# Branch transform of 64 by 32 points in place of 128 by 16, its first stage as pairs of matmuls of 64 rows

## The chip, the cores and the metric

The kernel runs on one core of one Trainium2 chip. The time is device microseconds of one execution; three runs of the kernel before gave 1190.42, 1190.47 and 1191.18 us (median 1190.47). The engines are TensorE (PE; its weight loads are shown apart as PEld), VectorE (DVE), ScalarE (ACT), GpSimd (POOL) and SyncE (SP, which only issues transfers here). Everything is computed in 32-bit numbers; matmul operands are split into a rounded part and a remainder, so that a product takes three matmuls (high by high, high by low, low by high).

## The reference

Two kinds of layers alternate, each added to its input `x` (2048 rows of 576 channels). The first is a Fourier transform over rows and channels, of which the real part is kept. The second, the branch, is a long convolution along the rows, done through a transform of twice the length:

```
def _B_ref(q, k, v, shift_k, ssm_k, ssm_D):
    ...
    kv = k_shift * v                      # short convolution of k (4 taps), times v
    kv_f = rfft(pad(kv)); kf_f = rfft(pad(ssm_k))
    y = irfft(kv_f * kf_f)[:S] + kv * ssm_D
    return q * y

x = A_x
x = x + _A_ref(_layernorm(x), ...)
x = x + _B_ref(_layernorm(x), B_k, B_v, B_shift_k, B_ssm_k, B_ssm_D)
x = x + _A_ref(_layernorm(x), ...)
x = x + _B_ref(_layernorm(x), B_k, B_v, B_shift_k, B_ssm_k, B_ssm_D)
```

The branch's convolution does not depend on `x`, only the gate `q` does. So the kernel computes `y` once, beside the first Fourier layer, and uses it twice.

## The kernel before

The Fourier layer (`layer`) runs over steps: for each block of 512 output rows (`tb`) and each of two matrices (`g`), 16 steps `k`. A step multiplies one 128-row slice of the normed input (tile `mats`) by a matrix slice of 128 by 512 that is loaded from `c_mat`, split by ScalarE (L94) and VectorE (L95) and used by 14 matmuls of 512 columns: three for each of four accumulators (`s`) and two for the remaining channels (`rm`). `load_c` asks for the slice of the step after next, so splits run two steps ahead.

The branch (`branch`, a generator) is advanced by hand between half steps, up to step `F1_END` = 42 in its first stage. Its transform of the 2048 points (odd frequencies of the double length) is worked out as 128 points by 16. Stage one (`f1_products`) takes, for each of 16 residues `j` and for each source `src` (1 the filter `ssm_k`, 0 the signal `kv`), a tile of 128 rows by 576 channels, split into two parts `xf`, and multiplies it by cosines and sines (`fc`, from `f1c`, 128 by 4 times 128: two outputs `c`, high and low part). Per half of the channels and per output there are three matmuls of 288 columns over 128 rows into one PSUM bank (`bank()`, a ring of three, name `bk`); ScalarE copies it out (L454) and the pair of outputs is stored to `t_d` in DRAM (L455). The signal's rows come from `convolve`, long VectorE operations on 1152 columns (L398, L403), which are spread over the items of stage one. The operands of stage one (`xf`, `fc`) lie in one tile, `f1r`; the constants come by POOL's queue (`load_fr`, L172), the first of them by SP and a ScalarE copy (L419, L420).

The middle stage (`mid_half` and the functions beside it) reads `t_d` in groups of 128 partitions, four outputs by 16 residues by real and imaginary part, does the 16-point transform, the product with the filter's transform and the inverse, and stores to `v_d`. The last stage (`i2_products`) reads rows of `v_d`, multiplies by `i2c` (six matmuls of 128 rows per half row) and stores `yb_d`. The order on each engine is the program's order as far as the scheduler of the framework leaves it; it moves instructions ahead of others where operands are late.

Of the kernel before, what the change touches and what calls it, by code (L numbers as in the profile page):

```python
# [10 lines left out]
F32 = mybir.dt.float32  # L11
FR = mybir.dt.float32r
AF = mybir.ActivationFunctionType
OP = mybir.AluOpType

P = 128
S = 2048
D = 576
J = S // P
TB = 4  # L20
NT = 512
HD = D // 2
NC = 4
REM = D - NC * P
EPS = 1e-5
# [16 lines left out]
MW = 504  # L42
# [25 lines left out]
def fnet_h3_kernel(ctx: ExitStack, tc: tile.TileContext, x, c_mat, w_re, w_im, k_pad, v, shift_k,  # L68
                   ssm_k, ssm_d, f1c, i2c, midc, out):
    nc = tc.nc  # L70
# [3 lines left out]
    dr = ctx.enter_context(tc.tile_pool(name="dr", bufs=1, space=bass.MemoryType.DRAM))  # L74

    def mm(ps, lhsT, rhs, first, last, more=False):
        nc.tensor.matmul(ps, lhsT, rhs, start=first, stop=last, skip_group_check=more)  # L77

    def bank():
        return psp.tile([P, NT], F32, tag="b", bufs=3, name="bk")  # L80
# [83 lines left out]
    anchor, made, rounded, pows, biased, halved, added, evac, parted, stored = [], [], [], [], [], [], [], [], [], []  # L164

    def load_after(dst, src):
        with tc.issue_after(anchor[-1]):
            return nc.sync.dma_start(dst, src).ins
# [31 lines left out]
        made.append(nc.vector.tensor_tensor(t[:, D + REM:], y[:, :NC * P], h[:, :NC * P], OP.subtract).ins)  # L200
        return t

    t_d = dr.tile([P, J, 2, 2, D], F32, name="t")
    v_d = dr.tile([P, J, 2, D], F32, name="vd")
    yb_d = [dr.tile([P, D], F32, name=f"yb{j}") for j in range(J)]
    xa_d = [dr.tile([P, D], F32, name=f"xa{j}") for j in range(J)]
    xb_d = [dr.tile([P, D], F32, name=f"xb{j}") for j in range(J)]
# [144 lines left out]
    def quads(v):  # L352
        return v.rearrange("p (a q) -> p a q", a=4)

    def branch():
        f1r = region_b(FR, "f1r")
        lay(f1r, 0, ("xf", 2 * D, 3), ("fc", 4 * P, 5))
        at = lay(flts, SC_AT + CRAW * NT, ("so", D, 4), ("land", D, 3))
        lay(flts, at, ("craw", NT, 1))
        f1f = region_a(F32, "f1f")  # L360
        ks = f1f[:, :KR * 2 * D]
        lay(f1f, KR * 2 * D, ("wt", 2 * D, 2), ("rp", 2 * D, 2))
        tmp = f1f[:, 8 * 2 * D:]
        wt, rows, landed, fcs = [], {}, {}, {}
# [8 lines left out]
        def load_k(upto):  # L373
            while k_loaded[0] < min(upto, (J + 4) // 2):
                i = k_loaded[0]
                at = i % KR * 2 * D
                nc.sync.dma_start(ks[:, at:at + 2 * D],
                                  bass.AP(tensor=k_pad.tensor, offset=k_pad.offset + 2 * i * D,
                                          ap=[[J * D, P], [1, 2 * D]]))
                k_loaded[0] += 1  # L380

        def k_rows(row):
# [28 lines left out]

        def f1_const(j):
            if j not in fcs:
                fcs[j] = quads(ring["fc"]())
                if pows:
                    load_fr(fcs[j], f1c[j])
                else:
                    raw = quads(tmp[:, :4 * P])
                    nc.sync.dma_start(raw, f1c[j])  # L419
                    nc.scalar.activation(fcs[j], raw, AF.Copy)  # L420

# [23 lines left out]
        def f1_products(j, src, xf, fc):  # L445
            for hf in range(2):
                so = two(ring["so"]())
                cs = slice(hf * HD, (hf + 1) * HD)
                for c in range(2):
                    ps = bank()  # L450
                    mm(ps[:, :HD], fc[:, c, :], xf[0][:, cs], True, False)
                    mm(ps[:, :HD], fc[:, c, :], xf[1][:, cs], False, False)
                    mm(ps[:, :HD], fc[:, 2 + c, :], xf[0][:, cs], False, True)
                    stored[:] = [nc.scalar.activation(so[:, c, :], ps[:, :HD], AF.Copy).ins]  # L454
                nc.scalar.dma_start(t_d[:, j, :, src, cs], so)  # L455
                yield

        conv, made_ops, split_up, share = convolve(), 0, [], 0.0
        for n, (j, src) in enumerate(todo):
# [3 lines left out]
            xf = f1_split(j, src)  # L463
# [48 lines left out]

        RW = D - MW
        per = MW // RW
        groups = P // 4
        mids = [(q, 1) for q in range(groups)] + [(q, min(per, groups - q)) for q in range(0, groups, per)]

        def width(n):
# [3 lines left out]
        def load_mid(n):  # L522
            if n < len(mids):
                first, count = mids[n]
                w = width(n)
                landed[n] = [r[:, :w] for r in apart] if n % 2 else [ring["land"]()[:, :2 * w]]
                ends = landed[n] if n % 2 else [two(landed[n][0])[:, i] for i in range(2)]
                src = t_d[4 * first:4 * (first + count)]
                if n < groups:
                    src = src.rearrange("q j c s d -> (q j c) s d")[:, :, :MW]  # L530
                    if n % 2:
                        for i in range(2):
                            load_after(ends[i], src[:, i])
                    else:
                        load_after(two(landed[n][0]), src)
                else:
                    src = src.rearrange("(g q) j c s d -> (q j c) s g d", q=4)
# [41 lines left out]
        def mid_inverse(n, yf):  # L579
            w = width(n)  # L580
            pv = bank()
            mm(pv[:, :w], mc[:, 2, :], yf[0], True, False)
            mm(pv[:, :w], mc[:, 2, :], yf[1], False, False)
            mm(pv[:, :w], mc[:, 3, :], yf[0], False, True)
            vo = ring["vo"]()[:, :w]
            act(vo, pv[:, :w], AF.Copy)
            first, count = mids[n]
            dst = v_d[4 * first:4 * (first + count)]
            if n < groups:
                nc.scalar.dma_start(dst.rearrange("q j c d -> (q j c) d")[:, :MW], vo)  # L590
            else:
                nc.scalar.dma_start(dst.rearrange("(g q) j c d -> (q j c) g d", q=4)[:, :, MW:],
                                    vo.rearrange("p (g d) -> p g d", g=count))

        landed, halves, fcs = {}, {}, {}
# [30 lines left out]
        def load_row(j):  # L626
            if j < J:
                landed[j] = ring["land"]()
                load_after(landed[j], v_d[:, j].rearrange("p c d -> p (c d)"))

        def load_fc(j):
            if j < J:
# [11 lines left out]
        def i2_products(hf, j, fc, vf):  # L644
            yo = ring["vo"]()
            ps = bank()
            for c in range(2):
                cs = slice(c * D + hf * HD, c * D + (hf + 1) * HD)
                mm(ps[:, :HD], fc[:, c, :], vf[0][:, cs], c == 0, False)
                mm(ps[:, :HD], fc[:, c, :], vf[1][:, cs], False, False)  # L650
                mm(ps[:, :HD], fc[:, 2 + c, :], vf[0][:, cs], False, c == 1)
            act(yo, ps[:, :HD], AF.Copy)
            nc.scalar.dma_start(yb_d[j][:, hf * HD:(hf + 1) * HD], yo)

        for j in range(3):
            load_fc(j)
# [7 lines left out]
        for j in range(J):  # L664
            vf, fc = halves.pop(j), fcs.pop(j)
# [132 lines left out]
    for n, whole in layer(get_x0, lambda j: x[:, j, :], done0, pending):  # L798
        if (whole or whole is not None and n % J < J - 1) and n <= F1_END:
            at = n if whole else n - 0.5  # L800
# [27 lines left out]
        m = n - PREP  # L828
# [132 lines left out]
    cs, done = {}, []  # L961
# [68 lines left out]
    for n, whole in layer(get_x1, lambda j: xb_d[j], done1, pending, 1):  # L1030
# [71 lines left out]
def _parts(a):  # L1102
    h = _r11(a)
    return h, _r11(a - h.astype(np.float64))


def _constants():
    p, q, j, r = np.arange(P), np.arange(P), np.arange(J), np.arange(J)
    n = (16 * p[None, :, None] + j[:, None, None]) * (4 * q[None, None, :] + 1) % 8192
    ang = 2 * np.pi * n / 8192  # L1110
    f1 = [_parts(np.cos(ang)), _parts(-np.sin(ang))]
    f1c = np.stack([f1[0][0], f1[1][0], f1[0][1], f1[1][1]], axis=2)
    at = ang.transpose(0, 2, 1)
    i2 = [_parts(np.cos(at) / S), _parts(-np.sin(at) / S)]
    i2c = np.stack([i2[0][0], i2[1][0], i2[0][1], i2[1][1]], axis=2)
    th = 2 * np.pi * (j[:, None] * r[None, :] % J) / J
    f2 = np.zeros((4, J, 2, 2, 4, J))
    i1 = np.zeros((2, 4, J, 4, J, 2))
    c, s = np.cos(th), np.sin(th)
    for a in range(4):  # L1120
        f2[a, :, 0, 0, a, :] = c
        f2[a, :, 1, 0, a, :] = s
        f2[a, :, 0, 1, a, :] = -s
        f2[a, :, 1, 1, a, :] = c
        i1[0, a, :, a, :, 0] = c.T
        i1[1, a, :, a, :, 0] = -s.T
        i1[0, a, :, a, :, 1] = s.T
        i1[1, a, :, a, :, 1] = c.T
    m = [*_parts(f2.reshape(P, P)), *_parts(i1.reshape(P, P))]
    return f1c, i2c, np.stack(m, axis=1)  # L1130


# [34 lines left out]
```

## Time and profile before

| | us |
|---|---|
| median of three runs | 1190.47 |
| profiled execution, its time | 1190.62 |
| profiled execution, its span | 1188.8 |
| TensorE busy | 1172.7 |
| VectorE busy | 814.3 |
| ScalarE busy | 614.6 |

The profile is of one execution. A page gives the busy time of each engine; views of the trace give groups of like instructions, stretches of the span, the chain of waits that ended last, and a timeline. A row such as `L77 PE MATMUL bk<-f1r` is a matmul issued by line 77 that writes `bk` and reads `f1r`. Busy times of matmuls overlap, as one is fed while the one before still comes out.

### The profile page before, as it was taken

To read this page: it belongs to the slowest core of one execution; us is meant where nothing else is said; L and a number is where in the kernel's file an instruction comes from. 1 tells how busy PE (TensorE), PEld (TensorE's weight loads), DVE (VectorE), ACT (ScalarE), POOL (GpSimd) and SP (SyncE) were. 2 spreads that over 40 slices of the span, in tenths; PEclk is the share of its full clock that TensorE was granted. 3 is DMA by queue.
4 is the path that set the end of the run, shared out by engine and by line. 5 is a ranking of instruction groups with operands and counts; after the bars stand their busy time and mean duration, and the time that the engine had idled before them with its cause. 6 is when DMAs were issued, how large, how long until landed. Compare 5 with 4: busy or idle time off the path is not lost.

```text
span 1188.8 us, 17284 instructions
## 1 busy us (share of the span) xinstructions
PE 1172.7 (99%) x6077; PEld 1013.5 (85%) x6077; DVE 814.3 (68%) x1335; ACT 614.6 (52%) x1106; POOL 66.2 (6%) x100
## 2 busy tenths in 40 slices
PE   7999999999999999999999999999999999999997
PEld 6888888887788888889988898888888888889997
DVE  7899794677677677753447765874775776874764
ACT  7965665466656566644535656634434435540200
POOL 2200000000000000001101111000000000001111
PEclk9999999999999999999999999999999999999999
DMA  9889898545576546459957786872582597696621
GB/s 338 295 266 308 262 297 251 187 151 183 176 236 200 176 137 181 116 160 295 294 164 260 241 262 216 263 261 72 179 315 82 159 326 274 199 335 201 217 94 41
DMA packets 153770, 257.71 MB, mean 217 GB/s; under 512 B 27601, under 2 KB 68817, under 8 KB 153682
## 3 DMA queue, kind: packets, MB, share of 16 engines
q1 hardware_dynamic: 113074, 205.58, 53.7%
q10 hardware_dynamic: 36000, 42.63, 10.3%
q0 software_dynamic: 4608, 8.39, 2.6%
q8 instruction: 48, 0.79, 0.3%
q14 instruction: 40, 0.33, 0.1%
HBM read 189.89 MB, written 66.65 MB: 216 GB/s over the span
## 4 chain that ended last, share of the span: by engine, by line
PE 95%; DVE 2%; DMA 1%; ACT 1%; issue 0%; POOL 0%; POOLq 0%; SPq 0%; DVEq 0%; ACTq 0%
PE s L77 54%; PE bk L77 35%; PE rm L77 6%; DMA flts<-in_c_mat 1%; ACT flts L506 0%; DMA flts<-in_ssm_k 0%; DVE flts L183 0%; DVE u L95 0%; ACT mid L506 0%; DVE mats L95 0%; DVE mats L200 0%; ACT mats L197 0%; ACT u L94 0%; DVE mid L511 0%; POOL flts L186 0%
## 5 line engine op out<-in xcount | busy, mean ns | idle before, releaser
L77 PE MATMUL s<-mats 128*128 128x512 f32 x2088 | 524.1, 392 | 0.8 <-ACT mats L94 0.6
L77 PEld LDWEIGHTS s<-mats 128*128 128x128 f32 x2088 | 386.8, 188 | 79.8 <-DVE u L95 1.5
L95 DVE TENSOR_TENSOR mats<-flts,mats 128x512 fp32r<-128x512 f32 x201 | 137.5, 688 | 80.7 <-ACT mats L94 78.1
L94 ACT ACTIVATE mats<-flts 128x512 fp32r<-128x512 f32 x201 | 125.7, 627 | 102.5 <-PE bk L77 31.3
L506 ACT ACTIVATE flts<-bk 64x504 f32<-64x504 f32 (+3 forms) x180 | 99.0, 550 | 82.9 <-PE bk L77 76.4
L77 PEld LDWEIGHTS bk<-w,u 128*128 128x128 f32 x864 | 117.8, 188 | 4.7 <-ACT flts L506 1.3
L77 PE MATMUL bk<-w,u 128*128 128x288 f32 x864 | 120.5, 295 | 0.5 <-ACT flts L506 0.5
L77 PE MATMUL bk<-mid 128*128 128x504 f32 (+1 forms) x525 | 120.1, 356 | 0.7 <-ACT flts L506 0.2
L511 DVE TENSOR_TENSOR mid<-flts,mid 128x1008 fp32r<-128x1008 f32 (+3 forms) x90 | 80.3, 902 | 45.6 <-ACT mid L506 45.5
L77 PEld LDWEIGHTS bk<-mid 128*128 128x128 f32 x525 | 88.0, 188 | 16.7 <-ACT flts L506 1.8
L77 PE MATMUL rm<-mats 128*128 128x512 f32 x304 | 94.5, 390 | 0.0
L506 ACT ACTIVATE mid<-flts 128x1008 fp32r<-128x1008 f32 (+3 forms) x90 | 71.9, 799 | 37.2 <-DMA flts<-vd 14.2
L454 ACT ACTIVATE flts<-bk 128x288 f32<-128x288 f32 x128 | 50.7, 410 | 48.8 <-PE bk L77 48.3
L77 PE MATMUL bk<-f1r 128*128 128x288 f32 x384 | 64.7, 301 | 7.4 <-ACT f1r L94 6.8
L77 PEld LDWEIGHTS bk<-f1r 128*128 128x128 f32 x384 | 59.9, 192 | 13.9 <-ACT f1r L94 6.8
L77 PE MATMUL bk<-mats 128*128 128x288 f32 (+1 forms) x376 | 67.8, 317 | 0.0
L77 PEld LDWEIGHTS rm<-mats 128*128 128x128 f32 x304 | 57.0, 188 | 12.3
L77 PE MATMUL s<-t,mats 128*128 128x512 f32 x264 | 64.9, 389 | 0.0
L292 DVE TENSOR_TENSOR flts<-flts,bk 128x288 f32<-128x288 f32 x48 | 21.8, 453 | 61.5 <-PE bk L77 61.3
L77 PE MATMUL bk<-mats,t 128*128 128x288 f32 (+1 forms) x368 | 59.3, 303 | 0.0
L186 POOL TENSOR_TENSOR flts<-flts 128x1 f32<-128x1 f32 x35 | 30.1, 860 | 522.1 <-DVE flts L185 518.8
L77 PEld LDWEIGHTS bk<-mats 128*128 128x128 f32 x376 | 55.5, 188 | 3.4
(149 smaller groups left out, 1432.1 us busy)
## 6 DMA issues: line engine op xcount, KB each, us to landing
flts<-in_c_mat SPq DMA_DIRECT2D x148, 256.0 KB, 3.9
ph<-in_c_mat SPq DMA_DIRECT2D x54, 512.0 KB, 4.0
t<-flts ACTq DMA_DIRECT2D x64, 288.0 KB, 4.7
flts<-in_c_mat SPq DMA_DIRECT2D x30, 512.0 KB, 5.1
flts<-vd SPq DMA_DIRECT2D x16, 576.0 KB, 5.1
vd<-flts ACTq DMA_DIRECT2D x36, 252.0 KB, 2.9
flts<-t SPq DMA_DIRECT2D x16, 504.0 KB, 4.0
ud<-ph ACTq DMA_DIRECT2D x12, 512.0 KB, 5.3
```

The costliest lines, as they stand in the source:

```text
L77: nc.tensor.matmul(ps, lhsT, rhs, start=first, stop=last, skip_group_check=more)
L94: a = nc.scalar.activation(h, src, AF.Copy).ins
L95: return a, nc.vector.tensor_tensor(l, src, h.bitcast(F32), OP.subtract).ins
L186: pows.append(nc.gpsimd.tensor_tensor(rs, ve, mhalf, OP.pow).ins)
L292: added[:] = [nc.vector.tensor_tensor(rows[hf], rows[hf], ps[:, :HD], OP.add).ins]
L454: stored[:] = [nc.scalar.activation(so[:, c, :], ps[:, :HD], AF.Copy).ins]
L506: last_act.append(nc.scalar.activation(*args, **kw).ins)
L511: nc.vector.tensor_tensor(l, src, h.bitcast(F32), OP.subtract)
```

## The change

The 2048 points are worked out as 64 by 32. Stage one contracts 64 points for each of 32 residues `t`. Residue `j` lies on partitions 0 to 63 and residue `j` + 16 on partitions 64 to 127, so the tiles, their loads and their splits keep their size. For each of the two halves `b` three matmuls take 64 partitions of weights and data and yield 128 rows at once, 64 frequencies by real and imaginary part. The six matmuls are written in turns of `b` = 0 and 1, into two banks that are then copied out one after the other. `f1c` has half as many columns. The inputs `k_pad`, `v` and `ssm_k` are laid out for this on the host, `t_d` and `v_d` have the residue in another place, and the middle stage handles two frequencies by 32 residues by two parts in a group, with as many matmuls of the same shapes as before. In the last stage the constants have zeros in half of their columns, the rows of `v_d` are read in two pieces per partition, and `yb_d` is stored with even and odd rows apart.

```diff
+Q = P // 2
...
-    t_d = dr.tile([P, J, 2, 2, D], F32, name="t")
-    v_d = dr.tile([P, J, 2, D], F32, name="vd")
+    t_d = dr.tile([Q, 2, 2 * J, 2, D], F32, name="t")
+    v_d = dr.tile([Q, 2, 2 * J, D], F32, name="vd")
...
-        lay(f1r, 0, ("xf", 2 * D, 3), ("fc", 4 * P, 5))
+        lay(f1r, 0, ("xf", 2 * D, 3), ("fc", 2 * P, 5))
...
-                nc.sync.dma_start(ks[:, at:at + 2 * D],
-                                  bass.AP(tensor=k_pad.tensor, offset=k_pad.offset + 2 * i * D,
-                                          ap=[[J * D, P], [1, 2 * D]]))
+                nc.sync.dma_start(two(ks[:, at:at + 2 * D]), k_pad[:, 2 * i:2 * i + 2, :])
...
-                fcs[j] = quads(ring["fc"]())
+                fcs[j] = two(ring["fc"]())
...
-                    raw = quads(tmp[:, :4 * P])
+                    raw = two(tmp[:, :2 * P])
...
             for hf in range(2):
                 so = two(ring["so"]())
                 cs = slice(hf * HD, (hf + 1) * HD)
-                for c in range(2):
-                    ps = bank()
-                    mm(ps[:, :HD], fc[:, c, :], xf[0][:, cs], True, False)
-                    mm(ps[:, :HD], fc[:, c, :], xf[1][:, cs], False, False)
-                    mm(ps[:, :HD], fc[:, 2 + c, :], xf[0][:, cs], False, True)
-                    stored[:] = [nc.scalar.activation(so[:, c, :], ps[:, :HD], AF.Copy).ins]
-                nc.scalar.dma_start(t_d[:, j, :, src, cs], so)
+                ps = [bank() for _ in range(2)]
+                for n, (a, c) in enumerate(((0, 0), (0, 1), (1, 0))):
+                    for b in range(2):
+                        at = slice(b * Q, (b + 1) * Q)
+                        mm(ps[b][:, :HD], fc[at, a, :], xf[c][at, cs], n == 0, n == 2)
+                for b in range(2):
+                    stored[:] = [nc.scalar.activation(so[:, b, :], ps[b][:, :HD], AF.Copy).ins]
+                nc.scalar.dma_start(t_d.rearrange("q c (b j) s d -> (q c) j s b d", b=2)[:, j, src, :, cs], so)
                 yield
...
-        groups = P // 4
+        groups = Q // 2
...
-                src = t_d[4 * first:4 * (first + count)]
+                src = t_d[2 * first:2 * (first + count)]
                 if n < groups:
-                    src = src.rearrange("q j c s d -> (q j c) s d")[:, :, :MW]
+                    src = src.rearrange("q c j s d -> (q c j) s d")[:, :, :MW]
...
-                load_after(landed[j], v_d[:, j].rearrange("p c d -> p (c d)"))
+                load_after(two(landed[j]), v_d.rearrange("q c (b j) d -> (q c) j b d", b=2)[:, j])
...
-            nc.scalar.dma_start(yb_d[j][:, hf * HD:(hf + 1) * HD], yo)
+            nc.scalar.dma_start(yb_d[j].rearrange("(p b) d -> b p d", b=2)[:, :, hf * HD:(hf + 1) * HD], yo)
...
+    def halves(m):
+        return m.reshape(Q, 2, *m.shape[1:]).transpose(1, 0, *range(2, m.ndim + 1)).reshape(m.shape)
...
-        "k_pad": np.pad(a["B_k"][0], ((3, 1), (0, 0))),
-        "v": a["B_v"].reshape(P, J, D),
+        "k_pad": halves(np.pad(a["B_k"][0], ((3, 1), (0, 0)))[rows]),
+        "v": halves(a["B_v"].reshape(P, J, D)),
...
-        "ssm_k": a["B_ssm_k"].T.reshape(P, J, D),
+        "ssm_k": halves(a["B_ssm_k"].T.reshape(P, J, D)),
```

How this stands in the order on TensorE, first in the steady part of stage one (a half row between halves of a step; `bk` with a number is one use of a bank). Before:

```order
L77 MATMUL s0_66<-mats_70 128x512 x3
L77 MATMUL s1_67<-mats_70 128x512 x3
L77 MATMUL bk_948<-f1r_149 128x288 x3
L77 MATMUL bk_953<-f1r_149 128x288 x3
L77 MATMUL s2_68<-mats_70 128x512 x3
```

After:

```order
L78 MATMUL s0_66<-mats_70 128x512 x3
L78 MATMUL s1_67<-mats_70 128x512 x3
L78 MATMUL bk_948<-f1r_149 128x288
L78 MATMUL bk_949<-f1r_149 128x288
L78 MATMUL bk_948<-f1r_149 128x288
L78 MATMUL bk_949<-f1r_149 128x288
L78 MATMUL bk_948<-f1r_149 128x288
L78 MATMUL bk_949<-f1r_149 128x288
```

Three matmuls on one bank and three on the next have become three pairs, `bk_948` from the lower and `bk_949` from the upper half of the partitions; the matmuls of the transform around them are the same. The program has such a block at 72 places before and at 78 after.

A little earlier on TensorE, where the scheduler fills gaps, some groups do not stay pairs. Before:

```order
L77 MATMUL bk_810<-f1r_149 128x288
L77 MATMUL s0_66<-mats_70 128x512 x3
L77 MATMUL s1_67<-mats_70 128x512
L77 MATMUL bk_815<-f1r_149 128x288 x3
L77 MATMUL s1_67<-mats_70 128x512 x2
L77 MATMUL bk_835<-f1r_149 128x288 x3
L77 MATMUL s2_68<-mats_70 128x512 x3
L77 MATMUL bk_840<-f1r_149 128x288 x3
```

After:

```order
L78 MATMUL bk_810<-f1r_149 128x288
L78 MATMUL s0_66<-mats_70 128x512 x3
L78 MATMUL s1_67<-mats_70 128x512
L78 MATMUL bk_811<-f1r_149 128x288 x3
L78 MATMUL s1_67<-mats_70 128x512 x2
L78 MATMUL bk_835<-f1r_149 128x288 x3
L78 MATMUL s2_68<-mats_70 128x512 x3
L78 MATMUL bk_836<-f1r_149 128x288 x3
```

Here the order is as before: the three matmuls of the lower half (`bk_835`) and those of the upper (`bk_836`) stand apart, with matmuls of 128 rows between. Over the whole program 138 of the possible 192 pairs stand side by side.

On SP's queue at the start of the program, the first transfers before:

```order
L711 DMA early<-in_x 128x576
L419 DMA f1f<-in_f1c 128x512
L429 DMA flts<-in_ssm_k 128x576
L218 DMA flts<-in_c_mat 128x512
L711 DMA early<-in_x 128x576
```

After:

```order
L711 DMA early<-in_x 128x576
L428 DMA flts<-in_ssm_k 128x576
L418 DMA f1f<-in_f1c 128x256
L219 DMA flts<-in_c_mat 128x512
L711 DMA early<-in_x 128x576
```

The first filter rows are asked for ahead of the first constants, which are half as wide.

More of the change, by code (lines that the diff above doesn't have):

```diff
@@ L536, in load_mid @@
                 else:
-                    src = src.rearrange("(g q) j c s d -> (q j c) s g d", q=4)
+                    src = src.rearrange("(g q) c j s d -> (q c j) s g d", q=2)
                     for i in range(2):
@@ L587, in mid_inverse @@
             first, count = mids[n]
-            dst = v_d[4 * first:4 * (first + count)]
+            dst = v_d[2 * first:2 * (first + count)]
             if n < groups:
-                nc.scalar.dma_start(dst.rearrange("q j c d -> (q j c) d")[:, :MW], vo)
+                nc.scalar.dma_start(dst.rearrange("q c j d -> (q c j) d")[:, :MW], vo)
             else:
-                nc.scalar.dma_start(dst.rearrange("(g q) j c d -> (q j c) g d", q=4)[:, :, MW:],
+                nc.scalar.dma_start(dst.rearrange("(g q) c j d -> (q c j) g d", q=2)[:, :, MW:],
                                     vo.rearrange("p (g d) -> p g d", g=count))
@@ L646, in i2_products @@
             ps = bank()
[L647 to L651, printed above, removed]
+            for b in range(2):
+                cs = slice(b * D + hf * HD, b * D + (hf + 1) * HD)
+                mm(ps[:, :HD], fc[:, b, :], vf[0][:, cs], b == 0, False)
+                mm(ps[:, :HD], fc[:, b, :], vf[1][:, cs], False, False)
+                mm(ps[:, :HD], fc[:, 2 + b, :], vf[0][:, cs], False, b == 1)
             act(yo, ps[:, :HD], AF.Copy)
-            nc.scalar.dma_start(yb_d[j][:, hf * HD:(hf + 1) * HD], yo)
+            nc.scalar.dma_start(yb_d[j].rearrange("(p b) d -> b p d", b=2)[:, :, hf * HD:(hf + 1) * HD], yo)
         for j in range(3):
@@ L1107, in _constants @@
 def _constants():
-    p, q, j, r = np.arange(P), np.arange(P), np.arange(J), np.arange(J)
-    n = (16 * p[None, :, None] + j[:, None, None]) * (4 * q[None, None, :] + 1) % 8192
+    p, q, t = np.arange(Q), np.arange(Q), np.arange(2 * J)
+    n = (2 * J * p[None, :, None] + t[:, None, None]) * (4 * q[None, None, :] + 1) % 8192
     ang = 2 * np.pi * n / 8192
-    f1 = [_parts(np.cos(ang)), _parts(-np.sin(ang))]
-    f1c = np.stack([f1[0][0], f1[1][0], f1[0][1], f1[1][1]], axis=2)
+    f1 = np.stack([np.cos(ang), -np.sin(ang)], axis=-1).reshape(2, J, Q, P).transpose(1, 0, 2, 3)
+    f1c = np.stack(_parts(f1.reshape(J, P, P)), axis=2)
     at = ang.transpose(0, 2, 1)
[L1114 to L1118, printed above, removed]
-    c, s = np.cos(th), np.sin(th)
[L1120 to L1128, printed above, removed]
+    i2 = _parts(np.stack([np.cos(at), -np.sin(at)], axis=2).reshape(2, J, P, Q) / S)
+    i2c = np.zeros((J, P, 4, 2, Q))
+    for b in range(2):
+        for m in range(2):
+            i2c[:, :, 2 * m + b, b] = i2[m][b]
+    i2c = i2c.reshape(J, P, 4, P)
+    th = 2 * np.pi * (t[:, None] * t[None, :] % (2 * J)) / (2 * J)
+    f2 = np.zeros((2, 2, 2 * J, 2, 2, 2 * J))
+    i1 = np.zeros((2, 2, 2 * J, 2, 2, 2 * J))
+    c, s = np.cos(th), np.sin(th)
+    for a in range(2):
+        f2[a, 0, :, 0, a, :] = c
+        f2[a, 1, :, 0, a, :] = s
+        f2[a, 0, :, 1, a, :] = -s
+        f2[a, 1, :, 1, a, :] = c
+        i1[0, a, :, a, 0, :] = c.T
+        i1[1, a, :, a, 0, :] = -s.T
+        i1[0, a, :, a, 1, :] = s.T
+        i1[1, a, :, a, 1, :] = c.T
     m = [*_parts(f2.reshape(P, P)), *_parts(i1.reshape(P, P))]
-    return f1c, i2c, np.stack(m, axis=1)
+    return tuple(v.astype(np.float32) for v in (f1c, i2c, np.stack(m, axis=1)))
 def kernel(**inputs):
@@ L1141, in perm @@
         return m.transpose(1, 4, 3, 2, 0)
+    def halves(m):
+        return m.reshape(Q, 2, *m.shape[1:]).transpose(1, 0, *range(2, m.ndim + 1)).reshape(m.shape)
     f1c, i2c, midc = _constants()
+    rows = J * np.arange(P)[:, None] + np.arange(J + 4)
     arrays = {
```

## Prediction

> **What bounds the kernel now.** First the busy times of the page (engine, busy us, share of the span, instructions) and two rows of the span cut in 40 slices of 29.7 us (busy tenths).
>
> ```profile
> span 1188.8 us, 17284 instructions
> PE 1172.7 (99%) x6077; PEld 1013.5 (85%) x6077; DVE 814.3 (68%) x1335; ACT 614.6 (52%) x1106; POOL 66.2 (6%) x100
> PE   7999999999999999999999999999999999999997
> DVE  7899794677677677753447765874775776874764
> ```
>
> TensorE is at nine tenths or more in every slice but the first and the last, so whatever it is spared after the first slice should shorten the span, unless another engine then sets the pace. VectorE stands at 8, 9, 9 in slices 2 to 4, which are just where the branch's first stage runs. So I cut that stage into stretches (busy us and instruction counts; DMA share; GB/s), first all instructions, then only those that touch f1r, the tile of the first stage's operands.
>
> ```profile
> core 0: us, PE busy (x) PEld busy (x) DVE busy (x) ACT busy (x) POOL busy (x), PEclk, DMA share, GB/s
> 0.00:24.00 24.00, 17.22 (x73) 14.73 (x74) 18.07 (x60) 17.58 (x30) 6.43 (x14) 1.00 0.94 330
> 24.00:80.00 56.00, 55.35 (x269) 46.56 (x268) 48.07 (x93) 46.63 (x100) 10.60 (x12) 1.00 0.83 276
> 80.00:120.00 40.00, 40.00 (x214) 34.84 (x213) 39.64 (x46) 22.07 (x49) 2.12 (x4) 1.00 0.98 323
> 120.00:160.00 40.00, 40.00 (x220) 35.22 (x219) 32.25 (x38) 25.60 (x57) 2.12 (x4) 1.00 0.87 271
> 160.00:180.00 20.00, 20.00 (x110) 17.49 (x110) 19.96 (x24) 11.89 (x27) 0.53 (x1) 1.00 0.96 298
> 180.00:200.00 20.00, 20.00 (x111) 17.64 (x110) 8.30 (x12) 11.66 (x27) 0.00 (x0) 1.00 0.77 244
> ```
>
> The same with the filter on f1r:
>
> ```profile
> 0.00:24.00 24.00, 4.92 (x19) 4.30 (x19) 2.27 (x3) 3.34 (x5) 1.80 (x3) 1.00 0.94 330
> 24.00:80.00 56.00, 11.75 (x65) 10.24 (x65) 3.00 (x4) 3.36 (x5) 1.67 (x3) 1.00 0.83 276
> 80.00:120.00 40.00, 14.36 (x90) 13.66 (x91) 7.47 (x10) 5.47 (x9) 2.12 (x4) 1.00 0.98 323
> 120.00:160.00 40.00, 16.67 (x105) 15.71 (x105) 6.02 (x8) 5.75 (x9) 2.12 (x4) 1.00 0.87 271
> 160.00:180.00 20.00, 8.53 (x51) 7.98 (x51) 3.16 (x5) 3.10 (x5) 0.53 (x1) 1.00 0.96 298
> 180.00:200.00 20.00, 8.44 (x54) 8.03 (x54) 2.10 (x3) 1.35 (x2) 0.00 (x0) 1.00 0.77 244
> ```
>
> Three things are to be seen. TensorE is full from 24 us on (55.35 of 56, then all). All 384 first-stage matmuls (19 + 65 + 90 + 105 + 51 + 54) fall before 200 us. And VectorE is all but full beside it from 80 to 120 us (39.64 of 40) and from 160 to 180 (19.96 of 20). The granted clock is 1.00 throughout.
>
> What one matmul costs is the distance between starts, since busy times of pipelined matmuls overlap. The timeline of TensorE in the stage's steady part (start, length, operation):
>
> ```profile
> 100.87 0.96 PE L77 MATMUL bk<-f1r 128*128 128x288 f32 x6
> 101.67 1.55 PE L77 MATMUL s<-mats 128*128 128x512 f32 x6
> 103.06 0.95 PE L77 MATMUL bk<-f1r 128*128 128x288 f32 x6
> ```
>
> Six first-stage matmuls take 101.67 - 100.87 = 0.80 us, 0.133 us each; six of the transform 103.06 - 101.67 = 1.39 us, 0.232 each. Going from one kind to the other costs nothing that these starts show (0.232 for 512 columns and 0.133 for 288 are in proportion to the columns).
>
> **The matmuls.** Before, one half row is 2 outputs of 3 matmuls, each over 128 rows. Now it is again 2 outputs of 3, but each over 64 rows, one output fed by the lower partitions and one by the upper. The count stays 384, each still streams 288 columns and loads 128 columns of weights. So the change only pays where a matmul on the lower half runs at the same time as one on the upper half. No row of this trace has a matmul of 64 rows. The bounds: the second of a pair is free (saves 0.133), or it queues as now (saves 0). I take it as free, since the two share neither rows nor an output bank; the other end is a rival. Weight loads must keep up, two per 0.133 us instead of one. The trace bounds one load only from above, by the end of the kernel, where nothing but 288-column matmuls runs:
>
> ```profile
> 1080.00:1100.00 20.00, 20.00 (x153) 20.00 (x152) 9.49 (x21) 1.45 (x3) 2.11 (x2) 1.00 0.59 187
> ```
>
> 20 us over 153 is 0.131 per load and matmul, so a load takes between 0 and 0.131; I leave loads out of the sum, as they go to different rows.
>
> How many pairs there are is read from the change's own order on TensorE. The scheduler puts some groups of three on one half together, with nothing for the other half beside them. Counting neighbours on opposite halves gives 138 pairs, not 192: by the stretches above 5, 12, 45, 36, 15 and 25. The 133 after 24 us are worth 133 x 0.133 = 17.7 us of TensorE. By stretch TensorE needs, after the change, 56 - 1.6 = 54.4, 40 - 6.0 = 34.0, 40 - 4.8 = 35.2, 20 - 2.0 = 18.0 and 20 - 3.3 = 16.7 us.
>
> **What is late next: VectorE.** Its work is unchanged: 48.07, 39.64, 32.25, 19.96, 8.30. Every step of the transform waits for a split by VectorE, which stands in its queue behind the convolution's long operations; its matrices are loaded two steps ahead, and a step is to take 14 x 0.232 + 6 x 0.133 = 4.05 us, so the slack is some 8 us. From 80 to 120 us TensorE would need 34.0 and VectorE 39.64: 5.6 us come back as waits. From 160 to 180 the 2.0 us by which VectorE is longer fit in the slack, and it has 8.30 of 20 to do behind that. So between 17.7 (all carried over) and 17.7 - 7.6 = 10.1 (none) are kept; I take 17.7 - 5.6 = 12.1, as 40 us is much longer than the slack.
>
> **Entering and leaving 64 rows.** The 384 matmuls stand in 78 blocks among 128-row ones, 73 of them after 24 us, so the array changes its shape 146 times. The price is in no row. From below it is 0, as between the two streams above. From above, the groups of TensorE:
>
> ```profile
> L77 PE MATMUL bk<-f1r 128*128 128x288 f32 x384 | 64.7, 301 | 7.4 <-ACT f1r L94 6.8 <-ACT flts L454 0.7
> L77 PEld LDWEIGHTS bk<-f1r 128*128 128x128 f32 x384 | 59.9, 192 | 13.9 <-ACT f1r L94 6.8 <-ACT flts L454 1.3
> ```
>
> A matmul lasts 0.301 (its end is modelled) and its successor starts after 0.133, so its results come 0.168 after its stream. If the array had to empty, a change would cost 0.168, and with an unhidden weight load of 0.192 at most 0.36. I take 0, the nearest row being the change of streams above; the rest is the first rival. The Trainium skill speaks against me: TensorEngine Tiling (Array Packing), Tiling Modes, says that a change of tiling mode, not just of tile, drains TensorE. No run here shows it yet.
>
> **Evacuation and banks.** Two outputs now end together, and two of the three banks are held. ScalarE at that place:
>
> ```profile
> 103.65 0.81 ACT L454 ACTIVATE flts<-bk 128x288 f32<-128x288 f32 x2 [0.28 <-PE bk L77]
> 106.29 0.81 ACT L454 ACTIVATE flts<-bk 128x288 f32<-128x288 f32 x2 [1.83 <-PE bk L77]
> 106.99 0.62 ACT L94 ACTIVATE mats<-flts 128x512 fp32r<-128x512 f32 x1
> 107.51 0.68 ACT L94 ACTIVATE f1r<-flts 128x576 fp32r<-128x576 f32 x1
> 108.47 0.81 ACT L454 ACTIVATE flts<-bk 128x288 f32<-128x288 f32 x2 [0.28 <-PE bk L77]
> ```
>
> ScalarE waits 1.83 and 0.28 us a step for TensorE. With 0.40 less between two evacuations the 0.28 turns into 0.12 of lateness, the 1.83 into 1.43. Two copies take 0.81, so a bank is free some 0.5 us after its matmuls, and its next user comes after at least the 1.39 us of transform matmuls between. I cost it at 0; were it not covered, 0.12 at each of some 32 steps, 4 us, would be lost.
>
> **The loads.** The constants of the first stage halve. The chain of waits at the start (start, length, what), and below it the issue of these constants (count, KB each, us to landing):
>
> ```profile
> 1.66 4.36 DMA flts<-in_ssm_k
> ...
> 21.40 5.92 DMA flts<-in_c_mat
> ```
>
> ```profile
> f1r<-in_f1c POOLq DMA_DIRECT2D x15, 256.0 KB, 4.4
> ```
>
> The start hangs on transfers, at 330 GB/s by the first stretch. Four of these loads lie in it (three issues on POOL in the f1r row, one on SP), 4 x 128 KB less, 1.6 us at that rate if all of it were on the chain; and the first filter row is now issued ahead of the constants. Much of this chain is VectorE and ScalarE work that stays, so between 0 and 1.6 I take 0.5. That loads from vd come in two pieces of 2304 bytes and not one of 4608, and that t, yb and the inputs are laid out anew, I cost at 0 for want of any change in bytes; the row with two pieces of about this size now, and that with one:
>
> ```profile
> flts<-vd SPq DMA_DIRECT2D x16, 576.0 KB, 5.1
> ...
> flts<-t SPq DMA_DIRECT2D x16, 504.0 KB, 4.0
> ```
>
> lands no later for its size. The later stages keep their matmuls and their shapes; their constants differ in values only.
>
> **Sum.** The profiled run took 1190.62 us (span 1188.8), 0.15 above the median of 1190.47. 1190.6 - 12.1 - 0.5 = **1178.0**.
>
> **Rivals.** (1) Slower: the array empties at each change of shape. It costs 146 x 0.168 = 24.5 us at the least against 17.7 + 0.5 saved (VectorE then hides nothing, as TensorE is slower again): 1190.6 + 6.3 = 1196.9; with the weight load open, 146 x 0.36 = 52.6, 1225. It decides from (17.7 + 0.5) / 146 = 0.125 us a change. For it: 78 blocks are many, most of six matmuls only. Against: no wait between streams is seen today. This is where the skill's page would lead. (2) The pairs do not overlap and changes are free: only the loads remain, 1189 to 1190.6. For it: no row shows two matmuls at once. (3) Neither overlap nor free changes: 1190.1 + 24.5 to + 52.6, 1215 to 1243. (4) Changes cost some 0.11 to 0.14: a draw, 1188 to 1193. (5) VectorE's lag is carried over wholly: 17.7 + 0.5, 1172.4; this is within my forecast's range.
>
> **Chances.** Forecast with changes under 0.11: 0.44 (own range 1172 to 1188). Rival 1 0.31, rival 2 0.13, rival 3 0.07, rival 4 0.05. A measurement of this kernel tells 0.2% (2.4 us) from no change; faster 0.44, same 0.13 + 0.05 = 0.18, slower 0.31 + 0.07 = 0.38. The range from 1174 to 1213 leaves out rival 3, the upper part of rival 1 and the lowest of the forecast, about 0.19.
>
> **What would show it.** Starts of six first-stage matmuls spanning 0.40 us in place of 0.80, with the six transform matmuls behind them still at 1.39: pairs overlap, changes free. More than 1.39 plus a gap at each border: rival 1. Six still at 0.80: rival 2. VectorE full from 80 us on, with weight loads waiting for its splits of mats: the 5.6 us. First transform row earlier by about 0.5 us: the loads. I am wrong if TensorE's starts show gaps at the borders, or if after 200 us the gain is given back in a stage that I took as unchanged.

## The result, and the profile after

The changed kernel takes 1261.61 us (median of 4 runs, 1260.12 to 1262.22), the one before 1190.45: 1.0594 times as long, 95% interval 1.0576 to 1.0613, 71.2 us more. The predicted 1178.0 and its range to 1213 both missed it.

The page of the changed kernel first: the busy times, and in 40 slices of 31.5 us the busy tenths of TensorE, VectorE and ScalarE and the granted clock.

```profile
span 1259.4 us, 17283 instructions
PE 1208.0 (96%) x6077; PEld 1005.4 (80%) x6077; DVE 815.4 (65%) x1335; ACT 609.6 (48%) x1106; POOL 66.4 (5%) x100
PE   8999999999999999996677999999999999999997
DVE  7879785677776686622122676686577577784664
ACT  7955555466665576522222566644443444550110
PEclk9999999999999999998888999999999999999999
```

Two things are to be seen. In slices 19 to 22, some 567 to 693 us, every engine falls back at once and even the clock drops: here something outside the engines holds the kernel up. And where the prediction looked, in slices 2 to 7, TensorE is as full as it was.

The tile that stands in the middle of those four slices is `yb`, the output of the last stage. The view of one tile (count, ns of one issue as least/median/most, first and last start) shows its store on ScalarE's queue, changed first, before second:

```profile
L653 ACTq DMA_DIRECT2D yb<-flts x32: 488/2771/7935, 548.2 to 676.8; - x32
```

```profile
L653 ACTq DMA_DIRECT2D yb<-flts x32: 326/326/348, 534.5 to 611.5; - x32
```

Issuing a transfer took 0.33 us and now takes 2.77 at the median and up to 7.9. ScalarE can do nothing meanwhile. Its timeline in the changed kernel:

```profile
558.49 7.93 ACTq L653 DMA_DIRECT2D yb<-flts  x1
566.48 0.63 ACT L95 ACTIVATE mats<-flts 128x512 fp32r<-128x512 f32 x1 [8.01 <-issue]
```

The split of the transform's next slice (`mats`) stands behind the store, so TensorE waits too (in brackets, its idle time before the row):

```profile
564.07 3.77 PE L78 MATMUL bk<-w,u 128*128 128x288 f32 x27
577.21 3.25 PE L78 MATMUL bk<-mid 128*128 128x288 f32 x12 [4.29 <-DVE flts L293]
594.75 6.38 PE L78 MATMUL bk<-w,u 128*128 128x288 f32 x27 [3.75 <-ACT flts L506]
```

Behind such waits matmuls are slower as well: a like group of 27 takes 6.38 us in place of 3.77, at a granted clock of 0.68 from 590 to 600 us. The chain of waits passes through these stores and their landings (start, length, what):

```profile
596.91 17.61 DMA yb<-flts
...
619.33 15.86 DMA yb<-flts
```

The trace also holds the semaphore updates that tell of a landing. A store before gives 16 of them, the last 4.4 us after the issue began (median of the 32 stores, 1.7 to 6.8). A store now gives 3, the last after 14.7 us (7.0 to 19.9). The hold builds up: the first four issues take 0.49 to 1.07 us, the fifth 7.93.

In stretches (columns as in the prediction; before, then changed), TensorE's 60 us from 560 to 620 shrink to 44.50, at a clock of 0.86. The DMA engines are 0.54 busy on the mean of the 16, and were 0.74 busy before, so it is not their sum that runs out.

```profile
560.00:620.00 60.00, 60.00 (x362) 54.76 (x362) 22.95 (x27) 26.38 (x44) 4.23 (x8) 1.00 0.74 235
```

```profile
560.00:620.00 60.00, 44.50 (x215) 38.37 (x214) 11.65 (x12) 14.21 (x24) 4.22 (x8) 0.86 0.54 165
```

Now the first stage, where the gain was to be. TensorE's timeline over one step, and the row with which the step shown in the prediction (from 100.87) ended before:

```profile
109.82 1.66 PE L78 MATMUL s<-mats 128*128 128x512 f32 x6
111.41 0.67 PE L78 MATMUL bk<-f1r 64*128 64x288 f32 x6
112.01 1.64 PE L78 MATMUL s<-mats 128*128 128x512 f32 x6
113.49 0.61 PE L78 MATMUL rm<-mats 128*128 128x512 f32 x2
114.03 0.67 PE L78 MATMUL bk<-f1r 64*128 64x288 f32 x6
114.63 1.66 PE L78 MATMUL s<-mats 128*128 128x512 f32 x6
```

```profile
105.69 0.96 PE L77 MATMUL bk<-f1r 128*128 128x288 f32 x6
```

Six first-stage matmuls take 112.01 - 111.41 = 0.60 us, where they took 0.80. But the six of the transform behind such a block take 111.41 - 109.82 = 1.59 where they took 1.39, or 1.48 where the `rm` matmuls follow. A step takes 114.63 - 109.82 = 4.81 us, against 105.69 - 100.87 = 4.82 before: what the pairs save is lost at their borders (the changes between 64 and 128 rows), to 0.01 us. The view of weight loads shows the border itself, changed first, before second:

```profile
109.82 1.22 PEld L78 LDWEIGHTS s<-mats 128*128 128x128 f32 x6 [0.17 <-issue]
111.41 0.43 PEld L78 LDWEIGHTS bk<-f1r 64*128 64x128 f32 x6 [0.37 <-ACT mats L95]
112.01 1.22 PEld L78 LDWEIGHTS s<-mats 128*128 128x128 f32 x6 [0.16 <-issue]
```

```profile
100.64 0.95 PEld L77 LDWEIGHTS bk<-f1r 128*128 128x128 f32 x6
101.54 1.25 PEld L77 LDWEIGHTS s<-mats 128*128 128x128 f32 x6
```

Before, the first weight load of a group started ahead of its matmul, at 100.64 for 100.87 us. Now both start together, at 111.41 and at 112.01, and no load runs for 0.37 us on the way in and 0.16 on the way out. So a block of six breaks even. Over the whole stage the change costs time, since groups that the scheduler took apart pay borders without having a partner: of the 78 blocks in the trace 30 have three matmuls or fewer, and 30 x 2 x 0.2 = 12 us is an estimate of what they lose. The first read of `t` for the next stage's `mid` comes at 222.4 us in place of 210.0.

### The profile page after: what moved, and what is told of

Its sections match the earlier page's. It is cut to its first block, busy times and chain, and to the rows that moved or that the text cites. A ratio compares the mean times of both kernels' runs of the same rounds, so it can differ in the third digit from the quotient of the medians.

```text
span 1259.4 us, 17283 instructions
## 1 busy us (share of the span) xinstructions
PE 1208.0 (96%) x6077; PEld 1005.4 (80%) x6077; DVE 815.4 (65%) x1335; ACT 609.6 (48%) x1106; POOL 66.4 (5%) x100
## 3 DMA queue, kind: packets, MB, share of 16 engines
q0 software_dynamic: 4608, 6.42, 2.1%
## 4 chain that ended last, share of the span: by engine, by line
PE 44%; DMA 3%; ACTq 3%; DVE 1%; ACT 1%; issue 1%; POOL 0%; POOLq 0%; DVEq 0%; SPq 0%
PE s L78 27%; PE bk L78 15%; DMA yb<-flts 3%; ACTq L653 3%; PE rm L78 2%; DMA flts<-in_c_mat 0%; ACT mid L506 0%; ACT flts L506 0%; DVE u L96 0%; DMA xb<-gate 0%; DVE mats L96 0%; ACT mats L95 0%; DVE mats L201 0%; ACT u L95 0%; DVE flts L184 0%
## 5 line engine op out<-in xcount | busy, mean ns | idle before, releaser
L78 PE MATMUL s<-mats 128*128 128x512 f32 x2088 | 542.9, 401 | 8.1 <-DVE u L96 6.4
L78 PEld LDWEIGHTS s<-mats 128*128 128x128 f32 x2088 | 390.9, 191 | 102.6 <-issue 11.2
L78 PE MATMUL bk<-mid 128*128 128x504 f32 (+1 forms) x525 | 128.8, 373 | 26.8 <-ACT flts L506 14.1
L78 PEld LDWEIGHTS bk<-mid 128*128 128x128 f32 x525 | 93.0, 200 | 47.9 <-ACT flts L506 17.8
L78 PE MATMUL bk<-w,u 128*128 128x288 f32 x864 | 123.2, 299 | 3.8 <-ACT flts L506 3.8
L506 ACT ACTIVATE mid<-flts 128x1008 fp32r<-128x1008 f32 (+3 forms) x90 | 71.7, 797 | 30.6 <-PE bk L78 11.7
L454 ACT ACTIVATE flts<-bk 128x288 f32<-128x288 f32 x128 | 47.3, 408 | 64.1 <-PE bk L78 63.8
L78 PEld LDWEIGHTS rm<-mats 128*128 128x128 f32 x304 | 57.8, 190 | 12.9 <-issue 0.3
L78 PEld LDWEIGHTS bk<-f1r 64*128 64x128 f32 x384 | 35.5, 190 | 34.5 <-issue 15.1
L78 PE MATMUL bk<-f1r 64*128 64x288 f32 x384 | 54.7, 334 | 6.0 <-ACT f1r L419 5.5
```

The costliest lines, as they stand in the source:

```text
L454: stored[:] = [nc.scalar.activation(so[:, b, :], ps[b][:, :HD], AF.Copy).ins]
L506: last_act.append(nc.scalar.activation(*args, **kw).ins)
```

## The experiments

The theory after this: two causes. The store of `yb` makes up 71.2 - 12.4 = 59 us; the first stage 12.4, by borders of 0.2 us each that outweigh the pairs. Rivals: the slow stage has another cause (loads of `vd`, zeros in constants), and the first stage suffers from the layout or the banks and not from 64 rows.

**A plain store.** The last stage's constants get their columns in the order of the output rows, so nothing is left to be taken apart by the store.

```diff
-            nc.scalar.dma_start(yb_d[j].rearrange("(p b) d -> b p d", b=2)[:, :, hf * HD:(hf + 1) * HD], yo)
+            nc.scalar.dma_start(yb_d[j][:, hf * HD:(hf + 1) * HD], yo)
...
-    i2c = np.zeros((J, P, 4, 2, Q))
+    i2c = np.zeros((J, P, 4, Q, 2))
...
-            i2c[:, :, 2 * m + b, b] = i2[m][b]
+            i2c[:, :, 2 * m + b, :, b] = i2[m][b]
```

> The changed kernel with the columns of the last stage's constants in another order, so that its outputs come out in row order and yb is stored as one plain piece of 128 rows; all else as changed. Theory A (the 71 us are two things: the first stage, whose next stage begins 12.4 us later, and the store of even and odd rows, which blocks ScalarE's queue for 2.77 us at the median in place of 0.33): the store's issue goes back to 0.33 us, the clock stays at 1.00, and the time is 1190.5 + 12.4 = 1203, between 1200 and 1206. Rival B (the last stage is slow for its loads of vd in two pieces, or for zeros in its constants): it stays above 1235.

1203.77 us (1201.92 to 1205.13), 1.0111 times the kernel before, interval 1.0094 to 1.0128. The store's issue is back at 0.327 us and the mean clock at 0.999. So 1261.61 - 1203.77 = 57.8 us were the store's (one run further down changes the store alone and leaves the constants as they were), and the 13.6 us that are left are near the 12.4 of the first stage.

**Two stores of 64 rows,** even rows and odd rows, to the same places.

```diff
-            nc.scalar.dma_start(yb_d[j].rearrange("(p b) d -> b p d", b=2)[:, :, hf * HD:(hf + 1) * HD], yo)
+            for b in range(2):
+                nc.scalar.dma_start(yb_d[j].rearrange("(p b) d -> b p d", b=2)[b, :, hf * HD:(hf + 1) * HD],
+                                    yo[b * Q:(b + 1) * Q])
```

> The changed kernel with each store of yb as two transfers of 64 rows, even rows and odd rows, to the same places. Theory A1 (the store is slow because one transfer of two times 64 rows has a first dimension of 2): each transfer is issued in about 0.33 us, 64 of them cost ScalarE 21 us off the critical path, time 1202 to 1208. Rival A2 (rows with a gap between them are slow to write in DRAM, however they are issued): the issue still blocks for 2 us or more, time above 1235.

1207.61 us, ratio 1.0147 (1.0125 to 1.0168). The issue takes 0.512 us at the median, more than the 0.33 expected, and each store gives 16 updates again, the last after 3.7 us. The same rows with the same gaps are quick when they come as two transfers, so the gaps are not the cause.

**The store alone, in the kernel before.**

```diff
-            nc.scalar.dma_start(yb_d[j][:, hf * HD:(hf + 1) * HD], yo)
+            nc.scalar.dma_start(yb_d[j].rearrange("(p b) d -> b p d", b=2)[:, :, hf * HD:(hf + 1) * HD], yo)
```

> The kernel before, with only the store of yb changed to the form of the changed kernel (even and odd rows apart, so the rows of the branch's output land in another order). Theory A: the store alone costs what is not the first stage's, 71.2 - 12.4 = 59 us, so 1249, between 1240 and 1258. Rival B: it stays within 3 us of 1190.5.

This kernel keeps the old constants, so its rows land in an order that the next layer does not expect; the work is the same. 1246.85 us, ratio 1.0476 (1.0455 to 1.0497): 56.7 us for one line, and nothing else of the change is in it. The store gives 3 updates, the last after 14.7 us, as in the changed kernel. The issue:

```profile
L653 ACTq DMA_DIRECT2D yb<-flts x32: 488/2739/7372, 533.5 to 661.7; - x32
```

**More pieces.** The same line with rows taken 16 apart (`b=16`), and 4 apart (`b=4`); here too the rows land in another order.

> The kernel before, with the store of yb in the form of the changed kernel but with rows taken 16 apart, so that its first dimension is 16 and not 2 (the branch's rows land in another order). Theory A1 (a transfer's work is dealt out along its first dimension, and two pieces keep but few of the 16 DMA engines busy): with 16 pieces the store is about as quick as a plain one, issue about 0.5 us, time 1190 to 1197. Rival A2 (a store whose rows do not follow each other in DRAM is slow, or one whose two sides have different shapes): as slow as with two pieces, 1247, or slower, the gaps being wider.

> The same with rows taken 4 apart, a first dimension of 4. Theory A1: twice the DMA engines of two pieces, so the transfers that landed after 16 to 18 us on the chain land in about half of that, and the issue blocks far less: time between the plain store and the store of two pieces, 1192 to 1225. Rival A2: 1247, within 5 us.

With 16: 1190.12 us, ratio 0.9992 (0.9980 to 1.0004), no difference. With 4: 1201.40, ratio 1.0096 (1.0066 to 1.0125). The issues, 16 first, then 4:

```profile
L653 ACTq DMA_DIRECT2D yb<-flts x32: 525/525/639, 533.8 to 610.9; - x32
```

```profile
L653 ACTq DMA_DIRECT2D yb<-flts x32: 512/527/1382, 532.9 to 621.8; - x32
```

So one transfer of 128 rows costs by the first dimension of its pattern: 2 pieces add 56.7 us, 4 add 10.7, 16 nothing, though the rows lie further and further apart. That the pieces are dealt to as many DMA engines is the reading that fits. The trace does not name single engines, but the semaphore updates fit it: each store gives 3 with two pieces and 5 with four, which is the pieces and one more, and 16 with sixteen pieces as with a plain store. The last update comes after 14.7, 9.4 and 4.4 us at the median. With four pieces the issue is hardly held (1.4 us at most), so most of their 10.7 us must come by the late landing. The Trainium skill says how the work is dealt out: DMA: Bandwidth & Descriptors, Why a DMA increments its semaphore by 16 and not by 1, has a transfer use the largest number of engines up to 16 that divides the slowest dimension of both sides, which gives 2, 4 and 16 here. The runs agree, in rank and sign by their times and by number in the updates.

**Full rows.** The plain store, and first-stage matmuls over 128 rows with constants that are zero on the other half: the new split of the points without any matmul of 64 rows.

```diff
-                        at = slice(b * Q, (b + 1) * Q)
-                        mm(ps[b][:, :HD], fc[at, a, :], xf[c][at, cs], n == 0, n == 2)
+                        mm(ps[b][:, :HD], fc[:, 2 * a + b, :], xf[c][:, cs], n == 0, n == 2)
...
-    f1c = np.stack(_parts(f1.reshape(J, P, P)), axis=2)
+    f1p = np.zeros((J, 2, Q, 2, P))
+    for b in range(2):
+        f1p[:, b, :, b] = f1[:, b]
+    f1c = np.stack(_parts(f1p.reshape(J, P, 2, P)), axis=2).reshape(J, P, 4, P)
```

> As the run with the plain store, but the first stage's matmuls take all 128 rows, with constants that are zero on the other half (twice as many bytes of them, as before the change): 64 by 32 points, no matmul of 64 rows. Theory A with a price of 0.2 us at each border between 128 and 64 rows, which eats what the pairs save: no border, no pair, first-stage blocks of six at 0.80 us, and the time is that of the kernel before, 1189 to 1193. Rival C (the 12.4 us of the first stage come from the other layout or from two banks being held at once, not from 64 rows): it stays at 1200 or above.

1192.53 us (median of 9 runs), ratio 1.0027 (1.0016 to 1.0039). The layout, the two banks held at once, the two-piece loads of `vd` and the middle stage of 32 points together cost 2.3 us. In the profiled run, 1.5 us longer than the one before, all of it arises in or behind the last stage: the first store of `yb` is issued at 534.5 us in both, and the first matmul `s<-t,mats` of the next layer starts at 739.7 us in place of 738.2. So neither the two banks nor the first two stages' layout cost anything in that run; what costs it later is left open. The other 1203.77 - 1192.53 = 11.2 us are 64 rows: if the 138 pairs gain 18.4, the 156 borders cost 29.6, 0.19 us each.

**Borders without pairs.** Full rows, but the first output's three matmuls take only the 64 lower rows. Then the same in turns, 64 and 128, for more borders.

```diff
-                for n, (a, c) in enumerate(((0, 0), (0, 1), (1, 0))):
-                    for b in range(2):
-                        mm(ps[b][:, :HD], fc[:, 2 * a + b, :], xf[c][:, cs], n == 0, n == 2)
+                for b, at in enumerate((slice(0, Q), slice(0, P))):
+                    for n, (a, c) in enumerate(((0, 0), (0, 1), (1, 0))):
+                        mm(ps[b][:, :HD], fc[at, 2 * a + b, :], xf[c][at, cs], n == 0, n == 2)
```

> As the run on full rows (1192.5), but of each half row the three matmuls of the first output take only the 64 lower rows, and the three of the second all 128 (its constants are zero on the lower half): 140 borders between 64 and 128 rows, no pair that could run at once. Theory F (each border costs about 0.195 us, since (1203.8 - 1192.5 + 138 x 0.133) / 156 = 0.19): 140 x 0.19 = 27, so 1219 (1213 to 1226). Rival G (the borders are cheap, and the 11 us between those two runs are from something else, as from copies that come at once): 1192 to 1198.

> As the run before, with the matmuls of the two outputs in turns, 64 rows, 128 rows, 64 rows and so on: 312 borders and still no pair. Theory F (a price per border): 312 x 0.19 = 59, so 1252 (1240 to 1264). Rival H (a price per block, as for an emptied array once on the way in and once on the way out): within 8 us of the run before.

1216.85 us (ratio 1.0227, 1.0206 to 1.0247) with 140 borders: 24.3 us over full rows, 0.17 us each. 1253.30 (1.0533, 1.0512 to 1.0554) with 312: 60.8 us, 0.195 each. The price is paid at each border, in both directions, and not once for a block as rival H had it. TensorE in the first of them:

```profile
110.49 1.25 PE L78 MATMUL bk<-f1r 64*128 64x288 f32 x6
111.58 1.55 PE L78 MATMUL s<-mats 128*128 128x512 f32 x6
```

Six of these, none beside a partner, take 1.09 us: 6 x 0.133 = 0.80 and some 0.29 for a border inside and part of the one ahead.

**Other order of the pairs.** The plain store, with three matmuls on the lower half first and then three on the upper.

```diff
-                for n, (a, c) in enumerate(((0, 0), (0, 1), (1, 0))):
-                    for b in range(2):
-                        at = slice(b * Q, (b + 1) * Q)
+                for b in range(2):
+                    at = slice(b * Q, (b + 1) * Q)
+                    for n, (a, c) in enumerate(((0, 0), (0, 1), (1, 0))):
                         mm(ps[b][:, :HD], fc[at, a, :], xf[c][at, cs], n == 0, n == 2)
```

> As the run with the plain store (1203.8), but the six matmuls of a half row are written as three on the lower half, then three on the upper: as many borders to 128 rows (154 for 156), but 60 neighbours on opposite halves for 138. Theory D (two neighbours on opposite halves run at once): 78 pairs less, each worth 0.133 us, 10.4 us more, 1214 (1210 to 1218), and a block of six spans 5 x 0.133 + 0.2 = 0.87 us where it was 0.60. Rival E (a matmul of 64 rows is just quicker, about 0.07 us, whoever its neighbour is): 1203.8, within 2 us.

1203.23 us, ratio 1.0112 (1.0097 to 1.0127): no slower than in turns. That is the number of rival E, but its reason falls with the weight loads of the two runs, this one first, the run with borders second:

```profile
111.51 0.44 PEld L78 LDWEIGHTS bk<-f1r 64*128 64x128 f32 x6 [0.37 <-ACT mats L95]
```

```profile
110.49 0.43 PEld L78 LDWEIGHTS bk<-f1r 64*128 64x128 f32 x3 [0.36 <-issue]
111.08 0.43 PEld L78 LDWEIGHTS bk<-f1r 128*128 128x128 f32 x3 [0.16 <-issue]
```

Three loads on one half take 0.43 us, and six on both halves, three behind three, 0.44. In the first 0.12 us of that block two of its matmuls start:

```profile
111.52 0.41 PE L78 MATMUL bk<-f1r 64*128 64x288 f32 x2
```

A matmul of 64 rows is no quicker by itself; the two halves run at once, and the upper half starts although its matmuls are written after all those of the lower. The theory that only neighbours pair (D) was wrong in that point: as far as blocks of six show it, the count that matters is how many on both halves stand in one block.

**Fewer borders.** The plain store, with both half rows of an item written without a pause.

```diff
                 nc.scalar.dma_start(t_d.rearrange("q c (b j) s d -> (q c) j s b d", b=2)[:, j, src, :, cs], so)
-                yield
+                if hf:
+                    yield
```

> As the run with the plain store, but both half rows of an item are written without a pause, so that the scheduler may put twelve matmuls in one block: 104 borders in place of 156, 113 neighbours on opposite halves in place of 138 (the third bank makes some of them wait). Theory F: against full rows (1192.5) 104 x 0.19 - 113 x 0.133 = 4.7, so 1197, and up to some 10 us more where a block waits for a bank to be copied out. If borders cost nothing (rival G), 25 pairs less make it 3.3 us slower than the plain store, 1207.

1212.68 us, ratio 1.0190 (1.0173 to 1.0207), 6 us above the upper end of what was expected. The block of twelve:

```profile
114.17 1.82 PE L78 MATMUL bk<-f1r 64*128 64x288 f32 x12
115.33 0.43 PEld L78 LDWEIGHTS bk<-f1r 64*128 64x128 f32 x3 [0.33 <-ACT flts L454]
115.92 1.67 PE L78 MATMUL s<-mats 128*128 128x512 f32 x6
```

It spans 115.92 - 114.17 = 1.75 us and not 6 x 0.133 + 0.2 = 1.0: twelve matmuls need four banks, there are three, and the last three wait for ScalarE's copy of the first. In the first stage this wait about uses up what the fewer borders save: the last first-stage matmul starts at 212.4 us, with the plain store at 211.9, and the first store of `yb` is issued at 548.4 and 547.9. Most of the 9 us between the two runs are lost behind that: the next layer's first `s<-t,mats` starts at 761.3 us in place of 751.9. TensorE's longest wait there:

```profile
588.30 3.97 PE L78 MATMUL bk<-w,u 128*128 128x288 f32 x15 [4.04 <-ACT flts L507]
```

Just before, ScalarE waits 5.18 us for a load of `vd`, and from 580 to 600 us the granted clock is 0.83. Why the last stage waits in this run and not with the plain store, where no wait of TensorE behind the first stage exceeds 0.8 us, is left open. No version here beats the kernel before.

## Why the prediction was wrong, point by point

- **The step that failed is the last of the part on loads**: "That loads from vd come in two pieces of 2304 bytes and not one of 4608, and that t, yb and the inputs are laid out anew, I cost at 0 for want of any change in bytes". For `vd`, `t` and the inputs the full rows leave at most 2.3 us. For `yb` the bytes were the wrong measure: 57.8 us, four fifths of the result, come from the shape of the pattern (two pieces of 64 rows). The bound was taken from loads of two pieces within a partition, whose first dimension was still 128. (Of the two rows shown, the one with two pieces is `flts<-t`; `flts<-vd` was one piece.) What such a store does was seen in its landing, 14.7 us in place of 4.4, and in the hold of ScalarE's queue. No rival named it, and this step alone took the time out of the range.
- **Free changes of shape** ("I take 0") is a second step that failed, and it turned the sign of the first stage: the runs show 0.17 to 0.195 us a border, and 11.2 us were lost where 12.1 were to be won. The price lies in the bounds given (0 to 0.36), beyond the 0.125 from which rival 1 decides. The sentence of the Trainium skill on draining (TensorEngine Tiling (Array Packing), Tiling Modes), quoted against me, agrees with this price at each change. With the plain store the time is 1203.8, inside rival 1's 1196.9 to 1225: for the first stage the rival was the right theory, and that 1203.8 lies in the stated range is the rival's doing and not the forecast's.
- **The pairs are free**: right. Six matmuls stand at 0.60 us, 0.40 and a border. A row of this trace could not show that the order of writing does not matter.
- **138 pairs worth 18.4 us, 17.7 behind 24 us**: borne out in sum only: with it, the price of a border comes out at 0.19 us, and the runs without pairs give the same by themselves (0.17 and 0.195).
- **VectorE takes back 5.6 us**: not tested. With its borders TensorE stayed as slow as before, so VectorE did not become the bound.
- **Banks and evacuation at 0**: right for blocks of six, since full rows hold two banks as well and reach the last stage with no loss; the blocks of twelve wait for a bank where the cover is gone.
- **Start earlier by 0.5**: the first first-stage matmul starts at 5.5 us instead of 6.8, the first transform row at 8.4 instead of 9.2. Its worth in the end was not measured apart.
- **After 200 us nothing changes**: with the plain store this held to about 1 us (12.4 us late at the first read of `t`, 13.6 at the end). It failed through the store, and by some 11 us in the run with blocks of twelve (11.7 at the first read of `t`, 22.7 at the end).

## What to carry to other kernels

Read every rearranged transfer as the pattern that the queue will get, and look at its first dimension, not only at its bytes. A permutation that was moved into constants cost nothing that shows: from the first store of `yb` to the next layer's first `s<-t,mats` it is 204.0 us with the plain store and 203.7 before. Matmuls on the two halves of the rows do run at once, but here a block of six only broke even and a block of three on one half lost. Before rewriting, set the number of borders to 128-row work, times some 0.2 us, against the pairs. Where longer blocks need more banks at a time than there are, saved borders come back as waits, so whether longer blocks would pay was not shown.

## What the runs showed of the hardware that was not expected

Transfers of 144 KB, slow by nothing but a first dimension of 2, landed 14.7 us after their issue at the median in place of 4.4, and from the fifth on they held the issuing engine for up to 7.9 us. What decides when an issue is held was not tested. The two halves of the rows work like two queues: three matmuls that were written after three others started beside them. And where TensorE had gaps of several us, the granted clock was lower, 0.86 between 560 and 620 us in the changed kernel and 0.83 between 580 and 600 in the one with blocks of twelve, so that matmuls between the gaps were slower too. How much of the 57.8 us is this lower clock was not separated.
